# Retention pairs and a two-matmul block on one core: a decay folded into q's cast, copies and masks moved between engines, and a new order of all tasks

## The chip, the cores and the metric

The kernel runs on one core of one Trainium2 chip. The metric is the device time of one execution in microseconds (us). Of the kernel before, three runs are given, and one execution was profiled.

## The reference, cut to what matters

```python
# q, k, v: (8, 8, 576, 64) f32;  x: (4608, 512);  w_in: (512, 2048);  w_out: (2048, 512)
scores = (q @ k.T) / sqrt(64)
gamma  = 1 - 2 ** (-5 - head)                     # one for each head
Dmat   = where(i >= j, gamma ** (i - j), 0)
attn   = (scores * Dmat) @ v
x      = attn, heads side by side                 # a row for each token
h      = x @ w_in
out    = (maximum(h, 0) ** 2) @ w_out             # (4608, 512) f32
```

So there is a retention (attention without softmax, with a decay between positions i and j), and behind it two matmuls with a squared ReLU between them.

## The kernel before, in words

**Units and groups.** A sequence of 576 positions is cut into four chunks of 128 and a tail of 64. A unit is one chunk of one batch, or the tails of two batches; there are 36 units (0 to 35) and 18 groups (0 to 17) of two units. Units 0 to 7 are "pairs": two neighbouring chunks of the same batch, loaded and cast together. The other 28 take the ordinary path.

**The path of a pair** (`add_unit_pair` at L532, `add_ret_pair` at L606). SP loads k, q and v as f32 (L441, L444) into `pair_c` or `stage`. They are cast to f16: `kx` (L555), `qx` (L553, a plain copy that also sorts the columns) and `vx` (L548, multiplied by a decay). PE transposes kx and qx into PSUM (`psT`, L572), and the result is copied to SBUF as `kqT` (L589). Then come the scores (`psc`, four banks), four causal masks of 512 columns each that DVE applies on the way out of PSUM (`rx`, L626), the sums of v by k (`psS`), the state R that is carried on (add at L648, decay at L599), and the outputs (`psO`): `fo1` multiplies vx by rx, `fo2` adds what the state gives, with a `drain` of PE between its two halves. In the end DVE multiplies psO by the decay table `gam_full` and writes `xT`, one unit after the other (L713). All small matmuls of the retention are issued in the helper `quad`, so they have line L483.

**The path of the ordinary units.** k, q and v are loaded (L419 for q, in four DMAs; L422 and L425 for the rest), cast on POOL (L497 k, L512 and L508 q with its decay, L518 v), and k and q are transposed together by a DMA on SP's queue (L529), which writes `kqT`. Slots of every pool are limited: five for kqT, five for each kind of load. The scores, sums and outputs are again at L483, masks at L828, the copy to xT on ACT at L889.

**The two matmuls.** The first is at L1209 (`ph<-xT,w_in`), or at L1058 where a Strassen scheme with seven products is used; ReLU is at L1219, the square at L1226, L1228 or L1101. The second is at L1248 for group 0 and at L1304 (Strassen) for the others. The weights w_in and w_out come in four blocks each, cast to f16 by DMAs that POOL issues (L459, `add_weight`). The results leave by stores on SP (L1001).

**What sets the order.** Nothing is scheduled at run time. Every piece of work is a task with an engine, and the string `ORDER` (L16) lists the numbers of all tasks; each engine gets its instructions in that order, and each queue is worked off strictly from the front. `SLOTS` says which buffer each tile takes. `WARM` matmuls without a use (L392) fill PE's start, and NoOps ("fillers", L377) are spread over PE's queue as `PADS` and `FRONT` say. The loads follow the list `FIRST`: k, q and v of units 0 and 2, eight weight blocks, then units 4 and 6; the load of k for unit 4 also waits for the sixth weight block.

```python
        def fo2():
            inter(0)
            nc.tensor.drain()
            inter(1)
```

Of the kernel before, what the change touches and what calls it, by code (L numbers as in the profile page):

```python
# [183 lines left out]
def kernel(  # L184
# [13 lines left out]
    P = 128  # L198
# [136 lines left out]
    for hp in range(NP):  # L335
        nc.scalar.activation(out=gam_f[:, hp, :], in_=iota_f, func=ACTF.Exp, scale=lncol[:, hp:hp + 1])
# [1115 lines left out]
```

## Time and profile before

| What | us |
|---|---|
| median of 3 runs | 283.84 (283.61 to 285.06) |
| the profiled execution | 283.93 |
| its span in the trace | 281.98 |
| what lies around the span | 1.95 |
| PE (matmuls) busy | 273.1 (97%) |
| DVE, ACT, POOL busy | 198.0, 198.4, 100.9 |
| first matmul of the first layer (L1209) | starts at 17.08 |
| third block of w_in | has landed at 22.10 |
| last matmul | ends at 278.3 |

The busy time of PE says little here, because the warm-up matmuls and the waits inside a pipeline count as busy or are short. What matters is when PE stands still between two matmuls, and what ended that. A table of waits gives the wait's total, how often it occurred, and the longest. The timeline gives start, duration, engine, line and tile. "SPq" is SP's queue of DMA issues; a duration there is the time until the next issue could be made.

### The profile page before, as it was taken

To read this page: it belongs to the slowest core of one execution; us is meant where nothing else is said; L and a number is where in the kernel's file an instruction comes from. 1 tells how busy PE (TensorE), PEld (TensorE's weight loads), DVE (VectorE), ACT (ScalarE), POOL (GpSimd) and SP (SyncE) were. 2 spreads that over 40 slices of the span, in tenths; PEclk is the share of its full clock that TensorE was granted. 3 is DMA by queue.
4 is the path that set the end of the run, shared out by engine and by line. 5 is a ranking of instruction groups with operands and counts; after the bars stand their busy time and mean duration, and the time that the engine had idled before them with its cause. 6 is when DMAs were issued, how large, how long until landed. Compare 5 with 4: busy or idle time off the path is not lost.

```text
span 282.0 us, 11585 instructions
## 1 busy us (share of the span) xinstructions
PE 273.1 (97%) x4726; PEld 237.5 (84%) x4726; DVE 198.0 (70%) x405; ACT 198.4 (70%) x374; POOL 100.9 (36%) x133
## 2 busy tenths in 40 slices
PE   8989999999999999989999999999999999999994
PEld 3567767888899888979998889898989999999983
DVE  4783379988988568586757595777597777565662
ACT  5657977577578965857797775686888485887831
POOL 7560036353655251455264343365265310000000
PEclk9999999999999999999999999999999999999999
DMA  6999998799999799999979999889979840022114
GB/s 192 300 201 208 246 323 192 171 231 164 195 166 212 166 178 209 222 178 165 230 169 212 195 200 207 210 183 245 182 197 219 155 114 2 5 84 105 40 74 149
DMA packets 119154, 50.03 MB, mean 177 GB/s; under 512 B 94784, under 2 KB 113728, under 8 KB 119104
## 3 DMA queue, kind: packets, MB, share of 16 engines
q1 hardware_dynamic: 114560, 44.84, 74.3%
q0 software_dynamic: 4224, 4.19, 9.1%
q8 instruction: 39, 0.64, 1.0%
q10 hardware_dynamic: 320, 0.26, 0.4%
q14 instruction: 11, 0.09, 0.1%
HBM read 36.70 MB, written 9.44 MB: 164 GB/s over the span
## 4 chain that ended last, share of the span: by engine, by line
PE 63%; DMA 16%; SPq 10%; DVE 4%; POOL 2%; issue 2%; ACT 1%; POOLq 0%; DVEq 0%; ACTq 0%
PE po L1304 28%; PE ph L1209 15%; PE ph L1058 13%; DMA w_out<-in_moe_w_out_dram 5%; SPq L419 5%; DMA loads<-in_q_dram 4%; PE psO L483 3%; DMA pair_c<-in_v_dram 3%; SPq L441 2%; DMA stage<-in_q_dram 2%; DMA kqT<-kq 2%; DMA out_dram<-o 2%; SPq L422 1%; SPq L529 1%; PE psS L483 1%
## 5 line engine op out<-in xcount | busy, mean ns | idle before, releaser
L1209 PE MATMUL ph<-xT,w_in 128*128 128x256 f16 x640 | 83.0, 273 | 0.9 <-DVE xT L713 0.5
L1209 PEld LDWEIGHTS <-w_in 128*128 128x128 f16 x640 | 61.6, 98 | 9.5 <-DMA w_in<-in_moe_w_in_dram 0.5
L1219 ACT ACTIVATE gT<-ph 128x512 f16<-128x512 f32 x80 | 46.2, 597 | 15.6 <-PE ph L1209 15.5
L1304 PEld LDWEIGHTS <-gT 128*128 128x128 f16 x544 | 51.1, 98 | 6.0 <-issue 0.3
L1304 PE MATMUL po<-w_out,gT 128*128 128x256 f16 x272 | 44.8, 273 | 0.0
L1304 PE MATMUL po<-wT,stage 128*128 128x256 f16 x272 | 42.5, 273 | 0.0
L1304 PEld LDWEIGHTS <-stage 128*128 128x128 f16 x408 | 38.1, 98 | 4.6 <-issue 0.2
L1304 PE MATMUL po<-wT,gT 128*128 128x256 f16 x272 | 40.8, 273 | 0.2 <-DVE o L1330 0.2
L1226 ACT ACTIVATE gT<-gT 128x512 f16<-128x512 f16 x66 | 40.0, 631 | 0.4
L497 POOL CAST kq<-loads 128x512 f16<-128x512 f32 x28 | 19.2, 687 | 54.0 <-DMA loads<-in_k_dram 49.6
L1101 ACT ACTIVATE gT<-gT 128x1024 f16<-128x1024 f16 x32 | 33.6, 1059 | 2.7 <-DVE gT L1087 2.6
L512 POOL TENSOR_TENSOR kq<-loads,qexp 128x512 f16<-128x512 f32 x24 | 26.8, 1116 | 22.1 <-DMA loads<-in_q_dram 21.8
L1058 PEld LDWEIGHTS <-pair_c 128*128 128x128 f16 x512 | 32.6, 98 | 1.3 <-issue 0.2
L518 POOL TENSOR_TENSOR v<-loads,vdec_full 128x512 f16<-128x512 f32 x24 | 27.4, 1146 | 10.7 <-DMA loads<-in_v_dram 10.6
L1277 DVE TENSOR_TENSOR stage<-gT,stage 128x512 f16<-128x512 f16 (+1 forms) x51 | 27.9, 561 | 0.8
L1087 DVE CUSTOM_DVE_ANT_0 gT<-ph,parts 128x512 f16<-128x512 f32 x24 | 16.5, 688 | 15.5 <-PE ph L1058 8.1
L1058 PEld LDWEIGHTS <-w_in 128*128 128x128 f16 x384 | 24.7, 98 | 1.2 <-issue 0.4
L1087 DVE CUSTOM_DVE_ANT_0 gT<-ph,stage 128x512 f16<-128x512 f32 x24 | 16.4, 686 | 12.8 <-PE ph L1058 12.3
L1330 DVE TENSOR_TENSOR o<-po,u 128x256 f32<-128x256 f32 x33 | 13.9, 421 | 15.2 <-ACT u L1320 4.7
L889 ACT CAST xT<-psO 128x512 f16<-128x512 f32 x28 | 15.9, 588 | 11.3 <-PE psO L483 11.2
L1320 ACT COPY u<-po 128x256 f32<-128x256 f32 x34 | 12.7, 374 | 12.2 <-PE po L1304 11.4
L1304 PE MATMUL po<-w_out,stage 128*128 128x256 f16 x136 | 21.2, 273 | 0.0
(111 smaller groups left out, 421.8 us busy)
## 6 DMA issues: line engine op xcount, KB each, us to landing
out_dram<-o SPq DMA_DIRECT2D x32, 256.0 KB, 3.1
loads<-in_k_dram SPq DMA_DIRECT2D x24, 256.0 KB, 4.9
loads<-in_q_dram SPq DMA_DIRECT2D x96, 64.0 KB, 3.4
loads<-in_v_dram SPq DMA_DIRECT2D x24, 256.0 KB, 4.2
w_in<-in_moe_w_in_dram POOLq DMA_DIRECT2D x4, 512.0 KB, 8.1
w_out<-in_moe_w_out_dram POOLq DMA_DIRECT2D x4, 512.0 KB, 14.4
pair_c<-in_k_dram SPq DMA_DIRECT2D x2, 512.0 KB, 5.5
pair_c<-in_q_dram SPq DMA_DIRECT2D x4, 256.0 KB, 6.1
```

Of the source, the lines that this page charges most:

```text
L497: op(out=out_.rearrange("p (n b a d) -> p n b a d", n=2, b=2, a=2), in_=in_.rearrange("p (a n b) d -> p n b a d", n=2, a=2))
L512: nc.gpsimd.tensor_tensor(out=out_.rearrange("p (t a d) -> p a t d", t=4, a=2), in0=tile_of["q32", u].rearrange("p (a t) d -> p a t d", a= ...
L518: nc.gpsimd.tensor_tensor(out=t, in0=tile_of["v32", u], in1=vdec[kind].rearrange("p (h o) -> p h o", o=1).to_broadcast([P, H, D]), op=ALU. ...
L889: (nc.scalar.copy if X_ENG[c] == "ACT" else nc.vector.tensor_copy)(out=tile_of["x", g].rearrange("p n (s e r t) -> p e (n s) r t", s=n, e= ...
L1058: nc.tensor.matmul(out_[:, e], lhsT=left[:, m, fi * P:(fi + 1) * P], rhs=right()[:, m], start=fresh and e == 0 and m == 0, stop=m == HK - ...
L1087: nc.vector._custom_dve(TENSOR_ADD_SAT, out=g_at(s, h, j), in0=bank(j, x), in1=part_at[name].rearrange("p (e t) -> p e t", t=P), s0=3.4028 ...
L1101: nc.scalar.activation(out=t, in_=t, func=ACTF.Square)
L1209: nc.tensor.matmul(tile_of["ph", g, fb][:, j, :], lhsT=w_in16[:, m, fi * P:(fi + 1) * P], rhs=tile_of["x", g][:, m, :], start=(m == 0), st ...
L1219: nc.scalar.activation(out=tile_of["g", g][:, nf * fb:nf * (fb + 1), :], in_=tile_of["ph", g, fb], func=ACTF.Relu)
L1226: nc.scalar.activation(out=t, in_=t, func=ACTF.Square)
L1277: (nc.gpsimd if eng == "POOL" else nc.vector).tensor_tensor(out=S_(k)(sl), in0=in0(sl), in1=in1(sl), op=op)
L1304: nc.tensor.matmul(tile_of["pb", g, bank], lhsT=left(i), rhs=right[:, i, :], start=(start and i == 0), stop=(i == HF - 1), skip_group_chec ...
```

## The change

The same result is to be computed. The parts of the change:

- The order of units is new: units 0 to 7 are now the chunks 0 and 1 of batches 0 to 3, and the chunks 2 and 3 of these batches take the ordinary path. A pair therefore never carries a state in, and the additions and matmuls for it are gone from the pairs and appear in later groups.
- q's cast in a pair multiplies by a decay table `pair_dec`, which about ten small instructions on DVE, POOL and ACT make at the start. Units 0 and 2 cast q on DVE, units 4 and 6 on POOL. With this, xT needs no `gam_full`: it is a plain copy, done for one unit on ACT and for the other on DVE (units 0 to 3), or for both on ACT (units 4 to 7). The table and its four exponentials are gone.
- Of the four masks of a pair, two stay as they were. For the other two, ACT copies the scores to SBUF as f16, and DVE multiplies them there by a mask that is now f16, in one instruction of 1024 columns.
- The first transposed q goes to two PSUM banks, and ACT and DVE each copy one of them, in quarters.
- Both halves of the first vx are cast on DVE; POOL did one of them, between two issues of weights.
- The first block of w_in is loaded in two halves.
- `fo2`'s two halves are placed apart: the state's part that needs the other unit goes first, then a NoOp that waits for its last matmul stands where the `drain` stood. The last group's drain goes in the same way.
- There are six slots for kqT instead of five, 24 warm-up matmuls instead of 30, and `ORDER`, `SLOTS` and `PADS` are new. NoOps on PE rise from 626 to 858.

```diff
-    PADS = (41, 0, 0, 4, 86, 0, 0, 0, 11, 130, 82, 147, 48, 0, 0, 0, 0, 0, 0, 0, 0, 0, 0, 0, 0, 0, 0, 0, 0, 0)
+    PADS = (135, 108, 41, 30, 85, 0, 0, 0, 8, 125, 79, 145, 20, 0, 0, 0, 0, 0, 0, 0, 0, 0, 0, 0, 0, 0, 0, 0, 0, 0)
...
+    units += [("full", b, c) for b in range(4) for c in range(2)]
...
-        units += [("full", b, c) for c in range(4) for b in bs] if bp else [("full", b, c) for b in bs for c in range(4)]
+        units += [("full", b, c) for c in range(2 if bp < 2 else 0, 4) for b in bs]
...
-    LD, KQ, V16, SB, G, KT, RB = 5, 7, 5, 0, 3, 5, 4
+    LD, KQ, V16, SB, G, KT, RB = 5, 7, 5, 0, 3, 6, 4
...
+    head_x = const.tile([P, 1], FP32, name="head_x")
+    part_i = const.tile([P, 1], mybir.dt.int32, name="part_i")
+    nc.gpsimd.iota(part_i, pattern=[[0, 1]], base=0, channel_multiplier=1)
+    nc.vector.tensor_single_scalar(out=part_i, in_=part_i, scalar=3, op=ALU.bitwise_and)
...
+    for a in range(2):
+        nc.vector.tensor_scalar(out=pair_dec[:, a], in0=pair_pos, scalar1=pair_ln[:, a:a + 1], scalar2=None, op0=ALU.mult)
+    nc.scalar.activation(out=pair_dec, in_=pair_dec, func=ACTF.Exp, scale=-1.0)
...
-    mask2 = const.tile([P, 2, 8, 16], FP32, name="mask2")
+    mask2 = const.tile([P, 2, 8, 16], FP16, name="mask2")
...
-    gam_f = const.tile([P, NP, P], FP32, name="gam_full")
-    for hp in range(NP):
-        nc.scalar.activation(out=gam_f[:, hp, :], in_=iota_f, func=ACTF.Exp, scale=lncol[:, hp:hp + 1])
...
+    Q_ENG = {0: ("DVE", "DVE"), 2: ("DVE", "DVE"), 4: ("POOL", "POOL"), 6: ("POOL", "POOL")}
+    O_ENG = {0: ("ACT", "DVE"), 2: ("ACT", "DVE"), 4: ("ACT", "ACT"), 6: ("ACT", "ACT")}
+    WARM = 24
...
+        for lo, hi in ((0, 256), (256, 512)) if i == 0 else ((0, 512),):
...
-                        engines[eng](out=t.rearrange("p (t a d) -> p a t d", t=NP, a=2), in_=x)
+                        t = t.rearrange("p (t a d) -> p a t d", t=NP, a=2)
+                        (nc.vector if eng == "DVE" else nc.gpsimd).tensor_tensor(
+                            out=t, in0=x, in1=pair_dec[:, :, NP * e:NP * e + NP].rearrange("p a (t o) -> p a t o", o=1).to_broadcast([P, 2, NP, D]), op=ALU.mult)
...
+            if u == 0 and i == 1:
+                for e in range(2):
+                    both = []
+                    for s in range(2):
...
+                            (nc.vector.tensor_copy if e else nc.scalar.copy)(out=out_, in_=in_)
...
+                if e:
+                    def fp(a=a):
+                        nc.scalar.copy(out=rT[1][:, a].rearrange("p n i -> p (n i)"), in_=rT["ps", 1][a])
+                    copied.append(add("ACT", base + 5, 0.6, fp, deps=[t]))
+                    sched.free("ff", copied[-1:])
+                    continue
...
+        def fm1():
+            y = rT[1].rearrange("p a n i -> p (a n) i")
+            nc.vector.tensor_tensor(out=y, in0=y, in1=mask2[:, 1].rearrange("p (o t) r -> p o (t r)", o=1).to_broadcast([P, 2 * NP, P]), op=ALU.mult)
...
+        def fo2():
+            tile_of["psO", g] = banks("psO")
+            inter(1)
+            rT["last"] = quads[-1]
+
         def fo1():
-
-            tile_of["psO", g] = banks("psO")
+            behind(nc.tensor.nop(hint="order", nofuse=True), rT["last"])
...
-        def fo2():
             inter(0)
-            nc.tensor.drain()
-            inter(1)
...
-                nc.vector.tensor_tensor(
-                    out=tile_of["x", g][:, :, s * P:(s + 1) * P].rearrange("p n (r t) -> p n r t", t=8),
-                    in0=tile_of["psO", g][s].rearrange("p (n t r) -> p n r t", n=NP, t=8),
-                    in1=gam_f.rearrange("p n (r t) -> p n r t", t=8), op=ALU.mult)
+                if O_ENG[u][s] == "ACT":
+                    nc.scalar.copy(out=out_, in_=in_)
+                else:
+                    nc.vector.tensor_copy(out=out_, in_=in_)
```

On PE's queue the start reads, before: 14 warm-up matmuls, the transposes of k, 5 warm, the transposes of q, 6 warm, the scores, 4 warm, the sums of unit pair 0. After: 6 warm, the transposes of k, 4 warm, the transposes of q, 6 warm, the scores, 1 warm, the sums, and 7 more warm ones further on. The first matmuls with w_in now stand in blocks of 8, 8, 16 and 56 between the retention of the second pair; before they stood in blocks of 32 and 48. SP's queue holds 252 DMAs in both, in another order.

More of the change, by code (lines that the diff above doesn't have):

```diff
@@ L454, in add_weight, with fn @@
         fb = i % 4
-        def fn():
-            src, dst = ((w_in[:, fb * 512:(fb + 1) * 512].rearrange("(m p) f -> p m f", p=P), w_in16[:, :, fb * 512:(fb + 1) * 512]) if i < 4 else
-                        (w_out[fb * 512:(fb + 1) * 512, :].rearrange("(n p) m -> p n m", p=P), w_out16[:, fb * 4:(fb + 1) * 4, :]))
-            tile_of["w", i] = nc.gpsimd.dma_start(out=dst, in_=src)
-            if i == 0:
-                behind(tile_of["w", i], tile_of["load", "v", 0])
-        issue = add("POOL", -90 + i, 0.9, fn, deps=issues[-1:] or [loaded["v", 0]], lag=1.0 if issues else 0.0)
-        issues.append(issue)
-        t = add("SP", 0, 2.58, lambda: None, deps=last_load + [issue], after=3.0 + LAG.get(f"w{i}", 0.0))
-        last_load[:] = [t]
-        wcast[i] = [t]
+        wcast[i] = []
+        for lo, hi in ((0, 256), (256, 512)) if i == 0 else ((0, 512),):
+            def fn(lo=lo, hi=hi):
+                sl = slice(fb * 512 + lo, fb * 512 + hi)
+                src, dst = ((w_in[:, sl].rearrange("(m p) f -> p m f", p=P), w_in16[:, :, sl]) if i < 4 else
+                            (w_out[sl, :].rearrange("(n p) m -> p n m", p=P), w_out16[:, fb * 4:(fb + 1) * 4, :]))
+                tile_of["w", i] = nc.gpsimd.dma_start(out=dst, in_=src)
+                if i == 0 and lo == 0:
+                    behind(tile_of["w", i], tile_of["load", "v", 0])
+            issue = add("POOL", -90 + i + lo / 1000, 0.9, fn, deps=issues[-1:] or [loaded["v", 0]], lag=1.0 if issues else 0.0)
+            issues.append(issue)
+            t = add("SP", 0, 2.58 if hi - lo == 512 else 1.29, lambda: None, deps=last_load + [issue], after=3.0 + LAG.get(f"w{i}", 0.0))
+            last_load[:] = [t]
+            wcast[i].append(t)
     for x in FIRST:
@@ L539, in add_unit_pair @@
             for e in range(2):
-                eng = ("DVE" if (e if name == "v" else lead) else "ACT" if name == "k" and u >= 4 or u == 2 and name != "v" else "POOL")
+                eng = Q_ENG[u][e] if name == "q" else ("DVE" if lead or name == "v" and e else "ACT" if name == "k" and u >= 2 else "POOL")
                 def fc(name=name, e=e, eng=eng):
@@ L568, in ft @@
             def ft(i=i, name=name):
-                t = tile_of["psT", u, i] = ps_ff.tile([P, 2, NP, P], FP16, name="psT", tag="ff")
+                two = u == 0 and i == 1
+                ts = [ps_ff.tile([P, 2, NP, P], FP16, name="psT", tag="ff") for e in range(1 + two)]
+                tile_of["psT", u, i] = ts
                 for e in range(2):
                     for x in range(NP):
-                        nc.tensor.transpose(t[:, e, x, :], tile_of[name + "x", u][:, e, x * P:(x + 1) * P], ident)
-            t = add("PE", base + 2 + i, 0.45, ft, deps=xs[name], acq=("ff",), size=16)
+                        nc.tensor.transpose(ts[e * two][:, e, x, :], tile_of[name + "x", u][:, e, x * P:(x + 1) * P], ident)
+            t = add("PE", base + 2 + i, 0.45, ft, deps=xs[name], acq=("ff",) * (2 if u == 0 and i == 1 else 1), size=16)
             if name == "q":
@@ L576, in add_unit_pair, with fe @@
             es = []
+            if u == 0 and i == 1:
+                for e in range(2):
+                    both = []
+                    for s in range(2):
+                        def fe(s=s, e=e):
+                            out_ = tile_of["kqT", s][:, NP:].rearrange("p x (t r) -> p t x r", r=16)[:, NP * e:NP * e + NP]
+                            in_ = tile_of["psT", 0, 1][e][:, e].rearrange("p y (r x) -> p y x r", x=NP)[:, :, :, 16 * s:16 * s + 16]
+                            (nc.vector.tensor_copy if e else nc.scalar.copy)(out=out_, in_=in_)
+                        both.append(add("DVE" if e else "ACT", base + 4 + s / 2, 0.42 if e else 0.37, fe, deps=[t] + T["kqT", s][:1]))
+                        T["kqT", s].append(both[-1])
+                    sched.free("ff", both)
+                continue
             for s in range(2):
@@ L651, in fr2 @@
         def fr2(s):
             def f():
-                if s == 0:
-                    tile_of["R", g] = st_pool.tile([P, 2, NP * D], FP16, name="R", tag="R", bufs=RB)
-                decay(tile_of["R", g][:, s], tile_of["tmp", g][:, s] if s or carry else rT["sum"][s][:, 0:256], 1)
-            return f
-        chain = []
-        for s in range(2):
-            if s or carry:
-                chain.append(add("DVE", base + 5.5 + s, 0.42, fr1(s), deps=[t] + (chain[-1:] if s else [T["R", g - 1]]), acq=("stmp",)))
-                if not s:
-                    T["Rread", g - 1].append(chain[-1])
-                sched.free("ff", chain[-1:])
-            chain.append(add("DVE", base + 5.6 + s, 0.5, fr2(s), deps=[t] + chain[-1:], acq=() if s else ("R",)))
-            if s or carry:
-                sched.free("stmp", chain[-1:])
-            if not s and not carry:
-                sched.free("ff", chain[-1:])
-            T["R0" if not s else "R", g] = chain[-1]
@@ L670, in add_ret_pair @@
-        T["Rread", g] = []
+                if at == 0:
+                    tile_of["R", mid + s] = st_pool.tile([P, 2, NP * D], FP16, name="R", tag="R", bufs=RB)
+                decay(tile_of["R", mid + s][:, at], tile_of["tmp", g][:, 1] if s else rT["sum"][s][:, 0:256], 1)
+            return f
+        r0 = add("DVE", base + 5.6, 0.5, fr2(0), deps=[t], acq=() if at else ("R",))
+        sched.free("ff", [r0])
+        r1 = add("DVE", base + 6.5, 0.42, fr1, deps=[t, r0], acq=("stmp",))
+        sched.free("ff", [r1])
@@ L672, in inter @@
+        r2 = add("DVE", base + 6.6, 0.5, fr2(1), deps=[r1] + ([T["R", mid + 1]] if at else []), acq=() if at else ("R",))
+        sched.free("stmp", [r2])
+        T["R0", g], T["R", mid + 1] = r0, r2
+        if at == 0:
+            T["Rread", mid], T["Rread", mid + 1] = [], []
+        T["Rread", mid].append(r1)
         def inter(other):
@@ L675, in inter @@
                     s = a ^ other
[L676 removed]
+                    if s:
                         x = 2 * n + b
[L678 removed]
+                        put2(s, 4 * a + x, tile_of["R", mid][half(a), at, half(x)], kqT(s)[half(a), NP + x, :], a)
         def put2(s, h, lhsT, rhs, row):
@@ L732, with prev @@
     place_of = {units[u]: (group_of[u], u - groups[group_of[u]][0]) for u in range(NU)}
+    def prev(g):
+        kind, b, c = units[units_of(g)[0]]
+        return b // 2 * 2 + 1 if b < 4 and c == 2 else g - 1
     def states(u):
@@ L965, in add_ret, with fa @@
         else:
+            def fa():
+                emit_out1(g)
+                tile_of["last", g] = quads[-1]
             def fb():
-                emit_out1(g)
-                nc.tensor.drain()
+                behind(nc.tensor.nop(hint="order", nofuse=True), tile_of["last", g])
                 emit_out2(g)
-            t = add("PE", base + 24, 0.45 + 32 * QUAD * n, fb, size=64 * n + 1, deps=T["masked", g] + out1_deps(g),
-                    acq=("prO", "ff", "ff"))
+            t = add("PE", base + 23.9, 0.2 + 4 * QUAD * n, fa, size=16, deps=out1_deps(g), acq=("prO", "ff", "ff"))
+            t = add("PE", base + 24, 0.25 + 24 * QUAD * n, fb, size=48 * n + 1, deps=[t] + T["masked", g])
             after_outs(g, t, t, base + 27)
```

83 lines of the change are left out of this document (44 added, 39 removed), and 110 rows, old and new, of the table ORDER.

## The prediction

> **What bounds the kernel now.** I read the page first, then PE's waits, then the timelines of PE and SP.
>
> ```profile
> PE 273.1 (97%) x4726; PEld 237.5 (84%) x4726; DVE 198.0 (70%) x405; ACT 198.4 (70%) x374; POOL 100.9 (36%) x133
> PE   8989999999999999989999999999999999999994
> DMA  6999998799999799999979999889979840022114
> ```
>
> PE is the bound; DVE and ACT have 30% to spare. The DMA engines are loaded until some 225 us, then nearly idle. So a gain must shorten PE's work, start it earlier, or close gaps between matmuls. PE's useful work is the same in both kernels. The gaps, by cause:
>
> ```profile
> PE psc L483 <- DMA kqT<-kq: 1.3, 2, 0.9
> PE ph L1209 <- DVE xT L713: 0.5, 2, 0.3
> PE ph L1209 <- DMA w_in<-in_moe_w_in_dram: 0.3, 1, 0.3
> ```
>
> The largest is two waits of the scores for a transposed kqT (at 112 and 124 us). From the starts of the matmuls in the timeline I add what that view leaves out: 0.37 at 161.7, 0.18 and 0.14 at 182, 0.43 and 0.24 at 195, and 0.29 at each of five drains (14.4, 21.2, 48.4, 57.8, 239.8). The start, on PE:
>
> ```profile
> 1.25 5.65 PE L392 MATMUL warm<-wT 128*128 128x512 f16 x14 [1.25 <-DVE wT L255]
> ...
> 10.10 0.81 PE L483 MATMUL psc<-kqT 64*64 64x128 f16 x32
> 10.85 1.04 PE L392 MATMUL warm<-wT 128*128 128x512 f16 x4
> ...
> 17.08 3.65 PE L1209 MATMUL ph<-xT,w_in 128*128 128x256 f16 x32 [0.34 <-DVE xT L713]
> 20.66 0.64 PE L483 MATMUL psO<-rx,vx 64*64 64x128 f16 x32
> 21.13 0.68 PE L483 MATMUL psO<-kqT,R 64*64 64x128 f16 x16
> ```
>
> The first layer begins at 17.08 after DVE's last xT, does 32 matmuls, and stands at 22.15 because the third block of w_in lands at 22.10.
>
> **The start, step by step.** DVE makes `pair_dec` ahead of kx's cast: nine small instructions of 0.18 to 0.23 us (L308, L274), so 1.6 to 2.1, less eight memsets of lncol (0.5). kx's cast starts some 0.9 late, at 6.0 instead of 5.11. qx's two casts become multiplications: 0.69 each (L548 on DVE) instead of 0.42, +0.5, done at 8.6 instead of 8.1. The copies of the first kqT run side by side: before 0.59 on ACT, then 0.69 on DVE; after, two quarters on each, 0.37 each on ACT (L1320) and 0.35 to 0.42 on DVE (half of L589's 0.69; L1330): 0.5 won. So the scores could start at 10.1 as now. DVE then has both halves of vx (+0.68) ahead of two masks (0.62 apiece), ACT copies the other two banks (0.59 each, as L889), and one mask instruction of 1024 columns ends the chain. For that one the rows give 0.68 (L984, both in f16) to 1.37 (L1022); I take 0.75, nearest to L1277's 0.75, which has the same types. psO comes at 14.0 instead of 13.8. Then xT: before, vx (0.68) and two products (1.27) in a row; after, a copy on ACT (0.59) beside DVE's (0.69), DVE having first to multiply the next q (1.3). xT is ready near 16.0 instead of 17.0: 1.0 won. But the stretch that follows ends at the third block of w_in, landed at 22.10, with the same matmuls done: by this sum PE would be there at 21.1 and wait. The half block comes in time (the whole landed at 16.52); its extra issue costs POOL 0.8 (L459), and POOL loses a vx of 1.4. The blocks land 2 to 3.5 us apart, each issued long before, so an earlier issue should bring little. I count the start at **0**, bounds −1.0 and +1.4 (the clock, below).
>
> **The middle.** The scores' gate: two NoOps now wait where drains stood. Where the ordinary groups have such a NoOp already, the next matmul starts 0.11 to 0.15 later; a drain took 0.29. Two of the five lie ahead of the wait at 22.1; three count, 3 × 0.17 = **−0.5**. Behind that NoOp stand the products of rx and vx and so xT; the state's part is issued first, so its end is mostly past. On POOL, q's casts for units 4 and 6 go from 0.61 and 0.84 to about 1.12 each (L512; 1.41 at worst, L548): +1.6. It is hidden: PE has the second layer of groups 0 and 1 queued from 38 to 50 us, and POOL idles 1.9 between the two q's. Uncovered it would cost 1.6 once. ACT gets eight copies of scores and six of xT (14 × 0.59), and loses four exponentials (0.39), two qx (0.61) and a copy: about +6 of 282. DVE loses 16 instructions of 0.68, two additions and more, gets the rest, about −3. Neither bounds; covered by their 30%. Of 232 more NoOps, about 230 are fillers: with one or two between matmuls of 256 columns the starts stay 109 to 113 ns apart, as without. I take 0 (bounds 0 and +0.5).
>
> **The waits for kqT.** The lines of SP:
>
> ```profile
> 105.95 2.23 SPq L529 DMA_TRANSPOSE kqT<-kq  x1
> 108.22 3.11 SPq L419 DMA_DIRECT2D loads<-in_q_dram  x4
> ...
> 116.74 1.72 SPq L529 DMA_TRANSPOSE kqT<-kq  x1
> 118.50 0.58 SPq L422 DMA_DIRECT2D loads<-in_k_dram  x1
> 119.32 2.42 SPq L529 DMA_TRANSPOSE kqT<-kq  x1
> ```
>
> SP issues one DMA after the other; a transpose takes at least 1.23, on average 1.77, for it often stands at the front of the queue until POOL has cast, and holds all loads behind it. DMA's share was 1.24 while the weights streamed (20 to 30 us) and is 0.84 to 0.85 from 40 to 60: room. In the new order most transposes stand further back: unit 17's has one k or v load and four q loads more ahead of it and one store less. Their data is then cast when their turn comes, and the sixth slot keeps them from waiting for PE. So I expect the queue to run faster and the waits at 112 and 124 to go (−1.3), and of the other gaps (1.36, with 0.18 at 51 us: 1.54) half, as the whole order is new: −0.8.
>
> **Sum**: 0 − 0.5 − 1.3 − 0.8 = −2.6. Span 281.98 − 2.6 = 279.4; with the 1.95 around it 281.3. The median is 0.1 below the profiled execution: **281.2**.
>
> **Rivals.**
>
> *The transposes come too late (slower).* Place: SP's queue from 60 to 165 us. Mean time to the next issue from 40 to 226 us: k or v load 0.76, q load 0.66, store 0.75. At that pace unit 17's transpose comes 0.76 + 4 × 0.66 − 0.75 = 2.6 later, unit 25's (two k or v, four q and two stores more) 5.7 later. Unit 25's landed at 162.6, its scores started at 165.1: 2.5 to spare, so 3.2 lost, less 0.5 for drains: 286.6. It decides only if the queue keeps its pace: 18 transposes up to there times 0.54 of waiting is 9.7, so if less than a third of that goes. For it: the queue is also slowed by landings. Against it: the idle share of DMA.
>
> *The queue runs just as before (no change).* PE comes earlier to the scores of groups 8 to 10 and waits there: kqT for group 10 landed at 136.76 and its scores began at 136.75, with nothing to spare. Then only the last drain and some late gaps are won: 283.4.
>
> *The start at half clock (no change).* The first 14 warm-up matmuls take 5.65 us, 0.4 apart; four later ones are 0.22 apart, though the page shows a granted clock of 1.0 throughout. So until about 5.9 PE ran at half rate. Only 6 of them now stand ahead of the transposes of k: PE is done at 3.8 and then idle until 7.0. If full rate starts 4.7 of work later, 11.7, the transposes take 0.86 each instead of 0.45, ten warm-up matmuls 0.43 instead of 0.25 or so, and the scores start at 12.7. The chain behind, 1.0 shorter, then ends 1.4 late at 22.1 or so. But a late PE waits less at 112 and 124: +1.4 − 0.5 − 1.3 = −0.4, 283.4. The Trainium skill, "TensorE: Matmul & The Clock Gate", Part 1, says that full rate needs about 3.4 us of sustained activity in a free-running window; the trace agrees, 4.7 us after PE's start. By that rule the gap of 3.2 would bring this rival about, a microsecond earlier or later from run to run.
>
> **How the numbers follow.** Forecast 0.58, late transposes 0.18, same pace 0.13, half clock 0.11. "Faster" starts at −0.5% (282.4), about what a measurement of this kernel can tell from no change. Faster 0.58; same 0.23 (the two middle rivals, less a little); slower 0.19. The forecast's own range is 279.4 to 282.4. The range for all: down to −5.2 (the gaps 1.54, the three drains 0.87, kqT's waits 1.3, 1.0 at the start, and 0.5 of smaller waits in PE's view), 278.6; up to the half clock without relief at the waits, +0.9, 284.7. The late transposes stay outside.
>
> **What would show it.** Right: no wait of psc for kqT over 0.5 us between 100 and 170; transposes near 1.3 to 1.5 on SP; the first L1209 work (now L1256) at or before 17, its third stretch at or before 22.2. Wrong: kqT at the head of PE's waits (late transposes or same pace), or warm-up matmuls 0.43 apart beyond 9 us. I would be wrong as well if the new buffer order brought waits for slots that the trace of before can't show.

## The result and the profile after

The changed kernel takes **286.77 us** (median of 15 runs, 284.58 to 289.56), the kernel before 284.04 beside it: a ratio of **1.008, 95% interval 1.0051 to 1.011**. A second measurement (after_again, below) gave 1.0122 (1.0074 to 1.0171). So it is about 1% slower where 1% faster was forecast. Every ratio here is to the kernel before measured beside it, and leaves out executions more than 1.5% above the fastest of their kernel: one of after_again (313.5 us, at a granted clock of 0.853), but also seven of 12 of tr_early and two of 11 of best2, each time with the profiled one among them.

The profiled execution took 285.42 us, its span is 283.70 (before: 283.93 and 281.98), so there are +1.72 us to find. From its page, busy time, PE by slices, the clock and the DMA engines:

```profile
PE 273.6 (96%) x4720; PEld 236.8 (83%) x4720; DVE 200.6 (71%) x398; ACT 202.5 (71%) x384; POOL 104.2 (37%) x134
PE   5999999999999999999999989999999999999994
PEclk9799999999999999999999999999999999999999
DMA  6999998989988889999869898798998933010024
```

Nothing new bounds the kernel; PE loses busy share in the first slice, and its clock is down to 7 tenths in the second (7 to 14 us). PE's waits:

```profile
PE psT L594 <- DVE kx L577: 2.0, 1, 2.0
PE psc L503 <- DMA kqT<-kq: 1.4, 3, 0.9
PE psS L503 <- POOL vx L568: 0.4, 1, 0.4
PE ph L1256 <- DVE xT L755: 0.3, 1, 0.3
```

kqT is still there, with three waits instead of two; the one of the pairs' sums for POOL's vx (0.4, at 53 us) is new. In PE's timeline the front:

```profile
1.25 2.74 PE L410 MATMUL warm<-wT 128*128 128x512 f16 x6 [1.25 <-DVE wT L256]
6.02 0.87 PE L594 MATMUL psT<-ident,kx 128*128 128x128 f16 x8 [2.02 <-DVE kx L577]
6.72 1.27 PE L410 MATMUL warm<-wT 128*128 128x512 f16 x4
...
8.87 2.41 PE L410 MATMUL warm<-wT 128*128 128x512 f16 x6
11.21 0.64 PE L503 MATMUL psc<-kqT 64*64 64x128 f16 x32
...
16.76 1.03 PE L1256 MATMUL ph<-xT,w_in 128*128 128x256 f16 x8 [0.29 <-DVE xT L755]
```

Four warm-ups at 6.72 start 216 ns apart, those from 8.87 on 427 again. The first layer starts at 16.76 (before 17.08). What was the wait at 22.1 (after 32 of its matmuls) ends at 22.73, when the third w_in block has landed (22.69; before 22.10).

I cut the span in three: up to that point, from there to the end of the last matmul, and what follows.

| us | before | after | forecast |
|---|---|---|---|
| up to the third stretch of the first layer | 22.15 | 22.73 | 0 |
| from there to the last matmul's end | 256.16 | 256.83 | -2.6 |
| behind it | 3.67 | 4.14 | 0 |

In the middle I took from the distance of any two starts what the matmul takes undisturbed in these traces (109.2 ns for 256 columns, 55.8 for 128, 216 for 512, and 11.5 and 5.6 for the small 64 x 64 matmuls of the retention with 128 and 64 columns, called pieces below): 240.5 us in both kernels. The rest is 15.39 before and 16.07 after: waits for kqT 1.68 and 1.97, other gaps over 0.15 us 2.47 and 1.71, smaller gaps 11.24 and 12.40. That makes +0.29, -0.77 and +1.16. (These sums count a wait from start to start, so they come out up to 0.2 us a wait higher than the table of waits.)

The lines of SP that answer to those shown of before:

```profile
108.22 1.73 SPq L549 DMA_TRANSPOSE kqT<-kq  x1
110.00 0.57 SPq L440 DMA_DIRECT2D loads<-in_k_dram  x1
110.62 2.62 SPq L437 DMA_DIRECT2D loads<-in_q_dram  x4
113.35 1.24 SPq L549 DMA_TRANSPOSE kqT<-kq  x1
...
119.62 1.30 SPq L549 DMA_TRANSPOSE kqT<-kq  x1
```

Unit 25's transpose, before and then after:

```profile
157.56 1.29 SPq L529 DMA_TRANSPOSE kqT<-kq  x1
```

```profile
163.05 1.31 SPq L549 DMA_TRANSPOSE kqT<-kq  x1
```

The transposes shown are shorter, but over all 28 the mean fell only from 1.72 to 1.63 us, with 2.55 as the longest, and the queue is not faster: unit 17's comes 2.3 us later than before, unit 25's 5.5 later.

### The profile page after: what moved, and what is told of

Read it like the earlier page. It is cut to its first block, busy times and chain, and to the rows that moved or that the text cites. A ratio compares the mean times of both kernels' runs of the same rounds, so it can differ in the third digit from the quotient of the medians.

```text
span 283.7 us, 11809 instructions
## 1 busy us (share of the span) xinstructions
PE 273.6 (96%) x4720; PEld 236.8 (83%) x4720; DVE 200.6 (71%) x398; ACT 202.5 (71%) x384; POOL 104.2 (37%) x134
## 3 DMA queue, kind: packets, MB, share of 16 engines
q0 software_dynamic: 4752, 4.19, 9.2%
## 4 chain that ended last, share of the span: by engine, by line
PE 68%; DMA 16%; SPq 8%; DVE 2%; POOL 2%; ACT 1%; issue 1%; DVEq 0%; POOLq 0%
PE po L1351 30%; PE ph L1256 17%; PE ph L1105 16%; DMA w_out<-in_moe_w_out_dram 5%; DMA kqT<-kq 4%; SPq L437 3%; PE psO L503 3%; DMA pair_c<-in_q_dram 3%; DMA loads<-in_q_dram 2%; DMA stage<-in_v_dram 2%; SPq L459 2%; DVE stage L1324 1%; PE psS L503 1%; PE psc L503 1%; SPq L443 1%
## 5 line engine op out<-in xcount | busy, mean ns | idle before, releaser
L1256 PE MATMUL ph<-xT,w_in 128*128 128x256 f16 x640 | 84.7, 273 | 0.4 <-DVE xT L755 0.3
L1351 PE MATMUL po<-w_out,gT 128*128 128x256 f16 x272 | 46.8, 273 | 0.0
L1351 PE MATMUL po<-wT,gT 128*128 128x256 f16 x272 | 42.7, 273 | 0.0
L532 POOL TENSOR_TENSOR kq<-loads,qexp 128x512 f16<-128x512 f32 x24 | 27.6, 1153 | 19.9 <-DMA loads<-in_q_dram 19.4
L538 POOL TENSOR_TENSOR v<-loads,vdec_full 128x512 f16<-128x512 f32 x24 | 28.2, 1179 | 16.9 <-DMA loads<-in_v_dram 14.6
L1324 DVE TENSOR_TENSOR stage<-gT,stage 128x512 f16<-128x512 f16 (+1 forms) x51 | 31.1, 623 | 2.2 <-ACT gT L1273 1.6
L1351 PE MATMUL po<-w_out,stage 128*128 128x256 f16 x136 | 22.1, 273 | 0.0
L933 ACT CAST xT<-psO 128x512 f16<-128x512 f32 x28 | 15.3, 589 | 8.3 <-PE psO L503 8.2
```

Of the source, the lines that this page charges most:

```text
L532: nc.gpsimd.tensor_tensor(out=out_.rearrange("p (t a d) -> p a t d", t=4, a=2), in0=tile_of["q32", u].rearrange("p (a t) d -> p a t d", a= ...
L538: nc.gpsimd.tensor_tensor(out=t, in0=tile_of["v32", u], in1=vdec[kind].rearrange("p (h o) -> p h o", o=1).to_broadcast([P, H, D]), op=ALU. ...
L933: (nc.scalar.copy if X_ENG[c] == "ACT" else nc.vector.tensor_copy)(out=tile_of["x", g].rearrange("p n (s e r t) -> p e (n s) r t", s=n, e= ...
L1256: nc.tensor.matmul(tile_of["ph", g, fb][:, j, :], lhsT=w_in16[:, m, fi * P:(fi + 1) * P], rhs=tile_of["x", g][:, m, :], start=(m == 0), st ...
L1324: (nc.gpsimd if eng == "POOL" else nc.vector).tensor_tensor(out=S_(k)(sl), in0=in0(sl), in1=in1(sl), op=op)
L1351: nc.tensor.matmul(tile_of["pb", g, bank], lhsT=left(i), rhs=right[:, i, :], start=(start and i == 0), stop=(i == HF - 1), skip_group_chec ...
```

## The experiments

Theories: the front at half clock; the first weight block in two halves; late transposes; the tail's order; and, formed on the way, the NoOps and how PE's instructions arrive. The middle of one execution differs from the next by up to a microsecond and more, so ratios (12 runs mostly) and waits are read together. A profile shows one execution; where two ratios have intervals that overlap, their difference is not shown.

**The front: warm5, w0whole.**

```diff
 first warm-up task
-  1 matmul
+  6 matmuls
```

> The changed kernel with five more warm-up matmuls after its first one, so that PE is busy from 1.25 us up to k's transposes at 6.0 instead of idle for 2.0 us. Theory A (the clock): in the changed kernel the warm-ups at 8.87 to 10.6 start 427 ns apart and the half-clock stretch is what makes the front late; here they start 216 ns apart, the first score matmul falls from 11.2 to about 10.2, and the third stretch of first-layer matmuls (57 blocks) starts 0.5 to 1.0 us earlier than 22.73: time 0.5 to 1.0 us below the changed kernel. Theory B (the first weights): that stretch starts when the third weight transfer's block has landed (22.69), which no warm-up moves; the half-clock stretch goes, and 22.73 stays within 0.15, time within 0.2 of the changed kernel.

Measured: 1.0071 (1.0044 to 1.0098).

```profile
6.76 1.03 PE L411 MATMUL warm<-wT 128*128 128x512 f16 x4
...
8.74 1.46 PE L411 MATMUL warm<-wT 128*128 128x512 f16 x6
```

The clock stays up (six warm-ups in 1.46 instead of 2.41 us), the scores start at 10.12, the first layer at 16.29; yet the third stretch waits for its block, 22.17, and starts at 22.22. Theory B is right on what holds the start in this execution. And the 0.5 won there is lost behind: the last matmul ends at 280.38, 0.8 later than in the first profile.

```diff
-for lo, hi in ((0, 256), (256, 512)) if i == 0 else ((0, 512),)
+w_in block 0 in one transfer
```

> The changed kernel with the first w_in block fetched in one transfer, as in the kernel before; nothing else is changed. Theory B: the two halves move in smaller packets and hold up all blocks behind them; in one piece, blocks 1 and 2 land at about 19.4 and 22.1 instead of 20.12 and 22.69, the third stretch starts at about 22.2 instead of 22.73, and the time is 0.5 us below the changed kernel. Theory A: the blocks may land earlier, but the start is held by the half-clock front, so 22.73 stays within 0.15 or first-layer matmuls before it get later.

Measured: 1.0102 (1.0058 to 1.0146, 6 runs). With the second v landed at 13.62, as in warm5 (13.64), the third block lands at 21.52 instead of 22.17. That looks like 0.6 us for the halves (the page counts 4752 instead of 4224 packets for the same 4.19 MB), but the other traces do not bear it out: over the 11 traces with halves the third block lands at 21.34 to 22.69, on average 21.93, over the eight without at 21.45 to 22.41, on average 21.88; counted from the second v, where its landing is in the trace, best has 7.89 with halves and best2 8.50 without. So no cost of the halves is shown. And in this execution the warm-ups were 427 ns apart up to 8.2 us and again from 9.5, PE came late, and the third stretch started at 22.47. So the block and the late front hold the start in turn, and no gain at the end is shown for either edit: over eight profiles with this front (after, after_again and six variants) it starts at 21.41 to 22.73, on average 22.06; over six with the front of before at 21.80 to 23.41, on average 22.33.

**The tail: tail_b.**

```diff
 PE, last groups of the second layer
-C A C C B C B A B B A    (A: matmuls of the last output, B: of the one before, C: of the one before that)
+C C C B C B B B A A A
```

> The changed kernel with the last eight second-layer matmul groups in the order that the kernel before has: the groups of the last output but one first, then those of the last. Theory E (the tail's order): the first of DVE's last two sums starts about 0.4 us before the other instead of both at once behind PE, the stretch from the last matmul to the end of the span falls from 4.14 to about 3.75, and the time by 0.3 to 0.4 us. Rival: the stores' issues on two queues set the end either way, and the stretch stays at 4.1.

Measured: 1.0059 (1.0032 to 1.0085). DVE's last sums, in the changed kernel and then in tail_b:

```profile
279.38 0.76 DVE L1377 TENSOR_TENSOR o<-po,p 128x256 f32<-128x256 f32 x2 [2.20 <-PE po L1351]
```

```profile
278.99 0.42 DVE L1377 TENSOR_TENSOR o<-po,p 128x256 f32<-128x256 f32 x1 [1.76 <-PE po L1351]
279.65 0.42 DVE L1377 TENSOR_TENSOR o<-po,p 128x256 f32<-128x256 f32 x1 [0.23 <-PE po L1351]
```

Both outputs' last matmuls were interleaved, so two sums stood in a row behind PE. Apart, the stretch behind the last matmul is 3.74 (fix 3.72, best 3.80) against 4.12 to 4.14 in all kernels with the changed tail. So theory E is shown: 0.4 us of the loss.

**The queues: tr_early, old_queues, new_queues, stores_later.**

```diff
 SP
 q(18) T(16)
+T(17)
 store v(18)
-T(17)
 ...
+T(23) T(22)
 v(24) k(25)
-T(23) T(22)
 ...
 T(24)
+T(25)
 v(26) k(27) store
-T(25)
```

> The changed kernel with four DMA transposes moved forward in SP's order: unit 17's straight behind unit 16's (past one store and one load), units 22 and 23's past two loads, unit 25's straight behind unit 24's (past two loads and one store). Theory C (late transposes): the waits of the score matmuls for kqT at 112.8 (0.43), 153.0 (0.49) and 165.9 (1.05) go, and the time falls by 1.5 to 2.0 us from the changed kernel. Rival D (the casts or the loads behind set the same pace): the transposes issue 1.1 to 2.4 us earlier, but the loads that they pass land as much later, and waits of 0.5 to 1 us come back at the next units; time within 0.5 of the changed kernel.

Measured: 1.0033 (0.9996 to 1.007), but that is the ratio of five executions. All 12 go from 283.15 to 291.42 us with a median of 287.67, which is 1.016 of the 283.11 beside it, and the profiled one took 288.57. In its trace the waits at 112 and 153 are gone. In their place, from PE's waits between 100 and 200 us:

```profile
PE psS L503 <- POOL v L538: 3.3, 1, 3.3
PE psc L503 <- DMA kqT<-kq: 1.0, 1, 1.0
```

PE now stands at 122.5 for unit 19's kqT (1.2), and at 164.6 for the cast of unit 25's v: POOL does that behind unit 27's k, whose load was moved 0.8 back. Behind the 3.3 us the granted clock is 0.5 from 169.5 to 172.9. Theory C is right for two waits; for the sum this execution is worse than D expected. The five executions of the ratio have no profile, so what they wait for is not known.

```diff
-SP, POOL (units 8 to 35): order of the changed kernel
+SP, POOL (units 8 to 35): order of the kernel before
```

> The changed kernel in which SP works off its DMAs, and POOL its casts of units 8 to 35, in the order of the kernel before; PE, DVE and ACT keep the changed kernel's order, and the buffers of kqT, kq, v and o are dealt out anew to fit. Theory F (the new order of SP and POOL is the cause): transposes of units 16, 17, 22 to 25 issue within 1 us of the kernel before (102.1, 106.0, 146.5, 148.2, 154.1, 157.6), the waits for kqT at 153 and 166 go, and the time falls by 1.0 to 2.0 us from the changed kernel's, to a ratio of 0.998 to 1.003 against the kernel before. Rival G (the DMA stream paces the middle whatever the order): other waits of the same sum come in their place, PE's gaps behind 100 us stay at 10 us or more, and the ratio stays at 1.006 to 1.010.

Measured: 1.0061 (1.0028 to 1.0095). The kqT waits at 153 and 166 are gone, as theory F wants, but the ratio is the one of rival G: a wait of 1.7 us for DVE came at 73.9 and one of 0.9 at 194.6, which the profile puts to issue. new_queues is the reverse edit on the kernel before.

> The mirror image: the kernel before, with SP's DMAs and POOL's casts of units 8 to 35 in the changed kernel's order; PE, DVE and ACT keep the order of the kernel before. It keeps five slots for kqT, as a sixth does not fit in its memory, so some transposes may wait for a slot. Theory F: the scores wait for late transposes at 112, 152 and 166, 1.5 to 3 us in all, and the time rises by 1.0 us or more over the kernel before (ratio 1.004 or above). Rival G: the order of the queues matters little, ratio 0.998 to 1.003.

Measured: 1.0034 (1.0 to 1.0067). That lies between F and G. Its kqT wait is 0.4 (at 165); PE waits 1.5 for DVE and 0.9 for issue. The new queues cost 0.3% with the old orders of PE, DVE and ACT; the old queues under the new orders are 0.2% below the first measurement of the changed kernel and 0.6% below the second, with intervals that overlap. So the queues are not shown to be the whole cause in either direction; that their fit with PE's order counts is likely, not shown.

```diff
 SP, kernel before
-store store k(18) T(17) q(18) v(18) k(19) q(19)
+k(18) T(17) q(18) v(18) k(19) q(19) store store
```

> The kernel before with two stores of SP's queue (issued at 103.6 and 104.3) moved behind the q load of unit 19 (114.6); nothing else is changed. Theory C' (what stands ahead of the loads sets the waits for kqT): loads and transposes of units 17 to 19 come 1.0 to 1.7 us earlier, the waits at 112 (0.56) and 123 (1.12) go or halve, and the ratio is 0.995 to 0.998. Rival D: the waits come back at later units, or DVE and ACT wait for a slot of o behind the late stores; ratio 0.999 to 1.003.

Measured: 1.0144 (1.0091 to 1.0197). The waits for kqT at 112 and 123 went, as C' says; but all waits of this kernel between 100 and 120 us show what the two stores held:

```profile
DVE o L1330 <- DMA out_dram<-o: 6.3, 2, 6.0
PE po L1304 <- DVE o L1330: 4.3, 1, 4.3
```

The stores hold slots of o, DVE waits for a slot, PE for DVE: rival D, with 4.3 us where 1.3 was removed. While PE stood, its granted clock fell to 0.5 (114.9 to 121.8), so what PE did between the end of the wait (117.2) and 121.8 ran at half rate as well.

**NoOps: after_again, nofill, fill, fill_late, nopad, after_nopad.** after_again is the changed kernel itself.

> The changed kernel once more, unchanged, for a second profile and for times on the chip of the three others. If the first profile (third stretch of the first layer at 22.73, 256.83 us from there to the last matmul, 4.14 us behind it) is typical, each of the three comes back within 0.5; the kernels with its queues so far had 256.8 to 258.2 for the middle one, so I expect 257.5 within 0.8, and a ratio of 1.007 to 1.009.

Measured: 1.0122 (1.0074 to 1.0171); 22.03, 257.37 and 4.13 us. The middle is as expected, the ratio above its range. kqT costs 1.5 (153, 166), and at 100 us DVE and then PE show the wait that stores_later has:

```profile
102.18 0.42 DVE L1377 TENSOR_TENSOR o<-po,u 128x256 f32<-128x256 f32 x1 [4.91 <-DMA out_dram<-o]
```

```profile
102.66 1.03 PE L1351 MATMUL po<-wT,gT 128*128 128x256 f16 x8 [1.90 <-DVE o L1377]
```

It is a slot of o whose store stands late in the new SP order: 2.1 us here, 0.5 to 0.8 in warm5, w0whole and tail_b, none in the first profile.

```diff
-PADS = (135, 108, 41, 30, 85, 0, 0, 0, 8, 125, 79, 145, 20, ...
+PADS = (41, 0, 0, 4, 86, 0, 0, 0, 11, 130, 82, 147, 48, ...
```

> The changed kernel with the fillers (NoOps between PE's matmuls) of the kernel before: 613 instead of 840, the difference all ahead of 100 us. Theory H (fillers cost time): in the changed kernel's trace, matmuls of 256 columns with two NoOps ahead are 115 to 118 ns apart on average instead of 109, the slow ones (144 to 211 ns) all at 73 to 77 us; without them these gaps go, 0.4 to 0.8 us, and the ratio falls to 1.002 to 1.006. Rival I: the NoOps are issued beside the matmuls, and the slow starts at 73 to 77 us have another cause (the clock, instruction fetching): they stay, and the time is within 0.3 of after_again.

Measured: 1.0081 (1.0049 to 1.0113). The slow starts at 73 to 77 us go (small gaps among large matmuls 0.40 instead of 0.77 to 1.09 us), but in their place PE stands 1.73 us, for nothing that the profile names, in the middle of a group's pieces:

```profile
73.22 0.19 PE L503 MATMUL psO<-kqT,R 64*64 64x64 f16 x1
75.14 0.19 PE L503 MATMUL psO<-kqT,Rm 64*64 64x64 f16 x1 [1.73 <-issue]
```

fill puts the changed kernel's PADS into the kernel before.

> The mirror image: the kernel before with the changed kernel's 840 fillers. Theory H: matmuls 144 to 211 ns apart appear somewhere between 60 and 90 us and the time rises by 0.4 to 0.8 us (ratio 1.0015 to 1.003). Rival I: ratio 0.999 to 1.001.

Measured: 1.0107 (1.0062 to 1.0151, 6 runs): 3 us, some four times the upper end of theory H. Large matmuls lose 2.0 us in small gaps (0.46 before). Half of that is at 75 to 78 us, where those with two NoOps ahead start 161 or 162 ns apart at a granted clock of 1.0; this part of theory H is borne out. And there is a stop of the same kind as in nofill:

```profile
88.03 0.28 PE L483 MATMUL psO<-rT,v 64*64 64x64 f16 x11
89.81 0.23 PE L483 MATMUL psO<-rT,v 64*64 64x64 f16 x5 [1.50 <-issue]
```

What arrives there is in the trace: one DMA queue is marked instruction, and its count follows PE's instructions. Its line in the page of before, of after and of nopad:

```profile
q8 instruction: 39, 0.64, 1.0%
```

```profile
q8 instruction: 40, 0.66, 1.0%
```

```profile
q8 instruction: 37, 0.61, 0.9%
```

Each packet has 16,384 bytes, and PE has 10,098, 10,317 and 9,549 instructions in these traces (matmuls, weight loads, NoOps and the like): at 64 bytes each that makes 39.4, 40.3 and 37.3 packets of 256 instructions. In nofill one ended at 73.7 and PE went on at 75.14, in fill at 88.4 and 89.81. So theory J: PE stops when the next packet comes late through the loaded DMA engines. The kept traces bear it out: in all 19 of them together, the profile puts 17 idle times of PE to issue that last 0.25 us or more and come after 18 us, and every one ends 193 to 195 instructions past a multiple of 256, counted from PE's first. fill_late has fill's number of NoOps, but behind 230 us, where the DMA engines are almost idle.

```diff
+        spread(227, between)    # behind the last ordinary scores
```

> The kernel before with 227 more fillers, as many as in the run fill, but all behind the last ordinary scores (from about 230 us), where the DMA engines are nearly idle. Theory J (instruction fetches): PE's instructions come in packets of 16 KB through the DMA engines, and PE stands when a packet comes late; where the engines are idle none is late, so no wait is added and the ratio is 0.998 to 1.002, against 1.011 for fill. Theory H (each filler costs issue time): the same number costs about the same, ratio 1.005 or above.

Measured: 1.0012 (0.9984 to 1.0039), no wait of that kind. So a NoOp does not cost the same everywhere, and theory H falls as a general rule; J is not contradicted. But behind 230 us there are also few pieces left (160 of the retention's small matmuls), so whether the idle DMA engines or the slower use of instructions spared PE is not separated. The next two drop all fillers behind the first 64, of the kernel before and of the changed one.

```diff
-PADS = (41, 0, 0, 4, 86, ...
+PADS = (0, 0, 0, 0, 0, ...
```

> The kernel before without any filler behind the first 64 (549 fewer). Theory J: fewer packets of instructions (36 or 37 instead of 39), but other places where they run out; waits that the profile puts to issue move or go, ratio 0.997 to 1.006, not to be told beforehand. Theory H: the time falls by 0.5 us or more.

> The changed kernel without any filler behind the first 64 (776 fewer). By theory J the slow starts at 73 to 77 us go and no wait of the kind of nofill's 1.9 us at 73 is likelier than with fillers; ratio 1.003 to 1.009, the waits for kqT at 153 and 166 staying. If the fillers were the whole cause of the slowdown, the ratio falls to 1.000.

Measured: 1.0043 (1.0011 to 1.0075) and 1.0127 (1.0091 to 1.0162). Neither is faster than the kernel whose fillers it lost. In nopad's trace a stop of 1.7 us for issue ends at 166.9, and from 167.2 to 170.6 the granted clock is 0.5: its large matmuls, with no NoOp ahead, start 213 ns apart there. PE's waits in after_nopad from 23 us on:

```profile
PE psO L503 <- issue: 3.0, 3, 1.3
PE ph L1256 <- issue: 1.1, 1, 1.1
PE psc L503 <- DMA kqT<-kq: 1.0, 1, 1.0
```

PE goes on 1.47, 1.25, 1.59 and 1.35 us after the end of a packet at 128.5, 156.3, 170.1 and 183.1. So fillers shift where a packet of 256 instructions runs out, and a place where PE uses them up quickly (a group's 64 x 64 pieces) is bad. The kernel before does best with its own PADS (0.4% better than with none, 1.1% better than with the other's); for the changed kernel none of the three is shown to be better. It keeps a loss of 0.3 to 0.6 at 73 to 77 us.

**Together: best, best2, fix, fix_w.** best is old_queues with the edits of warm5 and tail_b; best2 has those of w0whole and nofill as well.

> The kernel of old_queues with five more warm-up matmuls ahead of k's transposes and the last second-layer groups in the order of the kernel before. By theory F its three gains add up where nothing paces PE in the middle: 0.4 from the tail, and up to 0.5 from the start, so 0.4 to 0.9 below old_queues and a ratio of 0.995 to 1.000. By rival G the tail's 0.4 is won and the start's gain is lost again at the waits behind 100 us.

> All helpful edits on the changed kernel at once: queues of SP and POOL in the order of the kernel before, five more warm-up matmuls, the tail's order, the first w_in block in one transfer, and the fillers of the kernel before. If the causes found so far are all, and add (tail 0.4, fillers 0.5, queues 0.5 to 1, start up to 0.6), it is as fast as the kernel before or faster: ratio 0.996 to 1.001. If the order of PE's own work in the middle is a cause of its own, waits of PE for DVE and POOL stay behind 70 us and the ratio stays at 1.002 or above.

Measured: 1.0031 (0.9997 to 1.0064) and 1.0084 (1.0043 to 1.0125). best comes out 0.3% below old_queues, within overlapping intervals. In best2's profiled execution (290.24 us) PE stops for 3.3 us at 75.6, put to issue, and the granted clock is 0.5 from 79.0 to 82.4; whether its other executions have that stop is not known. fix removes the named waits in the changed kernel's own order, fix_w adds warm5.

```diff
 tr_early and tail_b, and
 POOL
+v(25)
 k(27)
-v(25)
 SP
+store(3)
 T(15) k(17)
-store(3)
```

> The changed kernel with five moves in its order: the four transposes of tr_early, unit 25's cast of v on POOL ahead of unit 27's cast of k (which waited for its load in tr_early and held the other 3.5 us), unit 3's store on SP ahead of unit 15's transpose (DVE waited for that slot of o at 100 us), and the tail's order of the kernel before. If these waits are the loss: waits at 100, 112, 153 and 165 go, one of up to 1.2 us at 123 stays, the middle is 255.5 to 256.5 us instead of 256.8 to 258.2, and the ratio 0.999 to 1.003 against the 1.008 and 1.012 measured for the changed kernel. If the load stream sets the pace all the same, new waits of 1 to 2 us come behind 165 and the ratio stays at 1.005 or above.

> As fix, with five more warm-up matmuls ahead of k's transposes. The clock stays up in the front; the third stretch still starts when the third weight block has landed, 21.4 to 22.7, so the time is within 0.5 us of fix. The ten more instructions of PE move the places where its packets of instructions end, which may bring or take a wait of 0.5 to 1.5 us of the kind that the profile puts to issue.

Measured: 1.0056 (1.0027 to 1.0084) and 1.0028 (0.9996 to 1.0059). In fix the waits at 100, 112, 153 and 165 are gone; PE's waits from 23 us on:

```profile
PE psc L503 <- DMA kqT<-kq: 2.3, 2, 1.5
PE psS L503 <- POOL vx L568: 0.4, 1, 0.4
PE po L1351 <- DVE stage L1324: 0.4, 1, 0.4
```

kqT again, at 123 (unit 19) and 194, and the middle takes 258.1 us, not the 255.5 to 256.5 hoped for. That fits the second branch, the load stream as the pace, better than the first. No version of the changed kernel is faster than the kernel before; best and fix_w can't be told from it.

## Why the prediction was wrong

The **step that failed** is "So I expect the queue to run faster and the waits at 112 and 124 to go (−1.3)": the waits for kqT came out 0.29 longer instead. The prediction had set the measure itself: 9.7 us of waiting at the head of SP's queue in the first 18 transposes, of which at least a third had to go. These 18 took 30.7 us instead of 32.0, so 1.35 went, a seventh. Nor did the queue run faster otherwise: between 100 and 170 us the k loads issue from 3.4 us earlier than before to 1.7 later, and the last transpose comes at 224.28 instead of 224.38. So the transposes that were placed behind more loads came 2.3 and 5.5 us later. That is what the rival *late transposes* had reckoned (2.6 and 5.7). Its price was too high, 3.2 for unit 25 alone: PE got there later as well, and the waits came to 0.43, 0.49 and 1.05 (at 113, 153 and 166 us). It was right about the queue and about the side, and had 0.18; that its 286.6 lies next to the measured 286.77 is luck, for most of the loss came from terms that it does not have. In tr_early, stores_later and fix, what was moved forward on SP pushed back something that PE then waited for.

The argument against it, the idle share of the DMA engines, was read in the wrong stretch. The prediction took 0.84 and 0.85 from 40 to 60 us and called it room. Between 60 and 170 us, where the transposes stand, the same trace of before has 0.83 to 1.33 in steps of 10 us, 1.04 on average; where the first wait builds up it is above the 1.24 of the streaming weights (the last three numbers are clock, DMA share and GB/s):

```profile
100.00:110.00 10.00, 10.00 (x236) 9.18 (x234) 7.94 (x19) 5.83 (x12) 2.31 (x4) 1.00 1.33 213
```

So no room was shown there, and the queue kept its pace.

Forecast and first profile are 4.3 us apart: 1.6 for kqT, 0.5 for the drains and other gaps, 0.6 for the start, 1.2 for small gaps and 0.5 for the tail.

Point by point, in the first profile:

- *The start, 0*: +0.58, within its bounds; over the profiles of all variants -0.3, so 0 was right. xT came early only where the clock stayed up (15.88 in tail_b, as reckoned; 16.76 here). The halved block was counted as "should bring little", and no effect of it is shown: the third block lands at 21.93 on average with halves, at 21.88 without.
- *Half clock*: the warm-ups 0.43 apart beyond 9 us came in the first profile and in w0whole, and not in tail_b: from run to run, as the rival said. The Trainium skill, "TensorE: Matmul & The Clock Gate", Part 1, says that the window runs free of the kernel; the spread agrees with it. No gain from removing it shows at the end (warm5: 1.0071, against 1.008).
- *Drains, -0.5, and half of the other gaps, -0.8*: together -0.77. At 48 and 57 us the gap at the former drain fell from 0.29 to 0.14; at the last group it rose from 0.29 to 0.32, so two counted and not three. A new gap stands against them: PE waits at 53 us for POOL's vx (0.58 from start to start, in this execution and in fix, not in after_again). POOL's casts of q took 1.3 to 1.5 each instead of the 1.12 reckoned; that they are the reason is not shown.
- *Fillers, 0 with bounds 0 and +0.5*: 0.3 to 0.6, at the upper bound; and in the kernel before the same NoOps at other places cost 1.1% (fill).
- *Not reckoned*: more small gaps where pieces and large matmuls meet and within pieces (+0.7), the tail (+0.47), and a slot of o, named only in general as "waits for slots".

Sum: +0.58 (start) + 0.29 (kqT) - 0.77 + 1.16 (small gaps, fillers in them) + 0.47 (tail) = +1.73. The medians differ by a microsecond more. Part of it is the wait for o, 0 to 2.1 us by profile. How the rest is shared out between kqT, o and packets of instructions in the runs without a profile stays open. Of the causes only the tail's 0.4 was removed with the effect foretold; the others are read from traces, and no edit brought the whole loss back.

## What to carry to other kernels

Where one queue feeds an engine that is busy 97% of the time, price a reordering by how many transfers stand ahead of each transfer that somebody waits for, at the queue's measured pace, and assume that this pace stays. A wait removed by moving one transfer forward was paid here by the ones that it passed: look for who waits for those, stores with their slots included. A new wait of PE can cost more than its length, for the clock may halve behind it. Look at the last groups by themselves: two outputs that ended together left two sums in a row behind the end, 0.4 us here.

## What the runs showed of the hardware

PE's program is fetched while it runs: 37 to 40 packets of 16 KB, through the DMA engines that carry the data. Where a packet was late PE stopped, 0.25 to 3.3 us here, always 193 to 195 instructions past a multiple of 256, and went on 1.2 to 1.6 us after the packet's end; the profile calls it issue. 227 more NoOps cost 1.1% ahead of 100 us, where the DMA share is 1.02 (fill, 25 to 100 us), and 0.1% (-0.2 to 0.4) behind 230 us, where it is 0.14 to 0.28 and few pieces run. The Trainium skill, "Trainium Architecture — The Big Picture", "The software stack", has 64 bytes for an instruction, which fits the counts, and streams that are brought in at load; here they come during the run.

A standing PE can lose its clock: behind waits of 1.7 (nopad), 3.3 (tr_early, best2) and 4.3 us (stores_later) the granted clock is 0.5 for 3.4 us, in stores_later for 6.8. Behind waits of 1.9 (after_again), 1.7 (nofill) and 1.5 us (fill) it stays at 1.0.
